# Cached attention on one core: from four 128-block tiles a head in five slots to three tiles of 172, 172 and 168 blocks in four

## The chip, the core and the metric

The kernel runs on one core of a Trainium2 chip. Five engines work side by side: TensorE (PE; its weight loads are listed as PEld), VectorE (DVE), ScalarE (ACT), GpSimd (POOL) and SyncE (SP). Here SP issues every load from HBM, in program order, and 16 DMA engines carry each one out. On-chip memory is SBUF, with 128 partitions, and PSUM, into which TensorE sums. The metric is the device time of one execution in microseconds, lower is better. The kernel before takes 2544.31 us, the median of three runs (2544.15 to 2545.1).

## The reference, cut to what matters

One token attends to a cache of 65,536 keys in each of 32 heads of 128 dimensions. A small feed-forward network runs beside it, and a sigmoid gate mixes the two.

```python
q = (x @ wq).reshape(B, Sq, H, Dh).transpose(0, 2, 1, 3)        # B = Sq = 1, H = 32, Dh = 128
scores = jnp.einsum("bhqd,bhkd->bhqk", q, k_cache) * (Dh ** -0.5)
p = _softmax(scores, axis=-1)
o = jnp.einsum("bhqk,bhkd->bhqd", p, v_cache)
a = o.transpose(0, 2, 1, 3).reshape(B, Sq, H * Dh) @ wo
b = (_silu(x @ w_gate) * (x @ w_up)) @ w_down                   # 512 -> 1792 -> 512
g = _sigmoid((x * gate_w).sum(-1, keepdims=True))
out = g * a + (1 - g) * b
```

All inputs are bfloat16. The two caches hold 32 x 65,536 x 128 x 2 bytes each, 537 MB; they are nearly all of the 1,087.6 MB that the kernel reads.

## The kernel before

**Tiles.** A head's 65,536 keys are 512 blocks of 128. A tile is `NB` = 128 blocks, so a head has `G` = 4 tiles for K and 4 for V, 4 MB each, and there are `N` = 128 tiles of each kind. A partition holds 128 consecutive keys of a tile, one contiguous run of 32,768 bytes in HBM and in SBUF. The function `big` hands out tiles from a pool of `SLOTS` = 5 slots. The load of a tile has to wait until whatever read the slot's last contents is done. `load` (lines 105 to 112) issues one transfer a tile; the last four V tiles go in two halves, the very last in pieces of 64, 32, 16 and 16 blocks (`CUTS`).

**Scores of a K tile.** `products` (210 to 227) is VectorE work, in place: one multiplication of the whole tile by the head's query (line 220), then three additions (line 224) that fold the 128 products of a key to 64, 32 and 16 columns. `scores` (229 to 241) lets TensorE sum the remaining `WIDTH` = 16 columns: 16 matmuls with an identity as weights, each over 128 numbers that lie 256 bytes apart, all into one slice of the PSUM tile `S_ps`, which holds the head's 512 blocks of scores.

**Softmax.** When a head's four tiles are scored, `row_max` (243) takes the maximum of each partition on VectorE, and a diagonal matrix and a matmul bring these maxima together; `exponentials` (253) takes the maximum over all, and ScalarE writes the weights `P_sb` and their sums. `total` and `weight` make the factor of the head.

**Values of a V tile.** `values` (276 to 289): 32 matmuls of four weight columns against 512 columns of V, summed into `O_ps`. `head_out` picks the diagonal out of it, `project` (326) multiplies with four heads' rows of wo, loaded in 512 KB pieces by `load_wo`.

**Order.** It is written by hand. The list `steps` (336 to 344) pairs each K tile n with a V tile v that comes four tiles behind; from `SPREAD` = 40 on, every fourth step leaves its V tile out until V is `LAG` = 8 tiles behind. In each step SP gets the load of K tile n and then of V tile v; VectorE gets the products of tile n, which at a head's first tile are cut into two halves, with `row_max` after the first instruction of the first half and `exponentials` after the second; TensorE gets the values of tile v and then the scores of tile n. At the start, wq and two K tiles are loaded, the queries are computed, then come the feed-forward weights in two slots and the first part of wo. The feed-forward itself is cut into three pieces in steps 1, 2 and 3. After the last step, `last_values` (291) works through the last V tile piece by piece, and the result is projected, cast and stored (389 to 399).

Of the kernel before, what the change touches and what calls it, by code (L numbers as in the profile page):

```python
# [15 lines left out]
NB = 128  # L16
SLOTS = 5
# [3 lines left out]
LAG = 8  # L21
SPREAD = 40

CUTS = (0, 64, 96, 112, 128)
# [3 lines left out]
def kernel(  # L28
# [23 lines left out]
    G = Sk // (NB * P)  # L52
    NBH = Sk // P
    N = H * G
    QG = 4
    assert Dh == P and Sk % (NB * P) == 0 and NBH <= 512 and H % QG == 0 and G >= 2
# [3 lines left out]
    ring = ctx.enter_context(tc.tile_pool(name="ring", bufs=SLOTS))  # L60
# [9 lines left out]

    def big(name):
        return ring.tile([P, NB * Dh], bf16, name=name, tag="big")

# [6 lines left out]
    wq_t = big("wq_t")  # L80
# [22 lines left out]
    K_tiles, V_tiles, S_tiles, P_tiles, O_tiles = {}, {}, {}, {}, {}  # L103

    def load(dst, cache, n, name, cuts=(0, NB)):
        h, g = divmod(n, G)
        t = big(name)
        view = t.rearrange("p (j d) -> p j d", d=Dh)
        src = cache[0, h, g * NB * P : (g + 1) * NB * P, :].rearrange("(p j) d -> p j d", j=NB)
        for a, b in zip(cuts[:-1], cuts[1:]):  # L110
            nc.sync.dma_start(out=view[:, a:b, :], in_=src[:, a:b, :])
        dst[n] = view
# [20 lines left out]


    gu_t = big("gu_t")
    wgu_sb = gu_t[:, : 2 * KT * F].rearrange("p (w t f) -> p w t f", w=2, t=KT)
    nc.sync.dma_start(out=wgu_sb[:, 0], in_=B_w_gate.rearrange("(p t) f -> p t f", t=KT))
    nc.sync.dma_start(out=wgu_sb[:, 1], in_=B_w_up.rearrange("(p t) f -> p t f", t=KT))
    wd_t = big("wd_t")
    wd_sb = wd_t[:, : FT * D].rearrange("p (t n) -> p t n", t=FT)  # L140
# [31 lines left out]
    def feed_forward_mid(gu_sb, eg):  # L172
        nc.vector.tensor_scalar_add(eg, eg, 1.0)
        nc.vector.reciprocal(eg, eg)
        hprod = consts.tile([P, FT], f32, name="hprod")
        nc.vector.tensor_tensor(out=hprod, in0=gu_sb[:, :FT], in1=eg, op=ALU.mult)
        hT = consts.tile([P, FT], bf16, name="hT")
        nc.vector.tensor_tensor(out=hT, in0=hprod, in1=gu_sb[:, FT:], op=ALU.mult)  # L178
        xg = consts.tile([P, KT], f32, name="xg")
        nc.vector.tensor_tensor(out=xg, in0=xT, in1=gwT, op=ALU.mult)  # L180
        xs = consts.tile([P, 1], f32, name="xs")
        nc.vector.tensor_reduce(out=xs, in_=xg, axis=AXIS.X, op=ALU.add)
        b_ps = psum_m.tile([1, D], f32, name="b_ps", tag="misc")
        for ft in range(FT):
            nc.tensor.matmul(  # L185
                b_ps,
                lhsT=hT[:, ft : ft + 1],
                rhs=wd_sb[:, ft, :],
                start=(ft == 0),
                stop=(ft == FT - 1),  # L190
            )
        g_ps = psum_m.tile([P, 1], f32, name="g_ps", tag="misc")
        nc.tensor.matmul(g_ps, lhsT=ones_f, rhs=xs, start=True, stop=True)
        eg2 = consts.tile([P, 1], f32, name="eg2")
        nc.scalar.activation(out=eg2, in_=g_ps, func=ACT.Exp, scale=-1.0)
        return b_ps, eg2
# [12 lines left out]

    def products(n, a=0, b=NB):  # L210

        h = n // G
        K = K_tiles[n][:, a:b, :]
# [15 lines left out]
    def scores(n):  # L229
        h, g = divmod(n, G)  # L230
        if g == 0:
            S_tiles[h] = psum_s.tile([P, NBH], f32, name="S_ps")
        for c in range(WIDTH):
            nc.tensor.matmul(  # L234
                S_tiles[h][:, g * NB : (g + 1) * NB],
                lhsT=ident_b,
                rhs=K_tiles[n][:, :, c],
                start=(c == 0),
                stop=(c == WIDTH - 1),
            )  # L240
        del K_tiles[n]
# [34 lines left out]
    def values(n):  # L276

        h, g = divmod(n, G)
        if g == 0:
            O_tiles[h] = psum_o.tile([4, 4 * Dh], f32, name="O_ps")  # L280
        for j in range(0, NB, 4):
            nc.tensor.matmul(  # L282
                O_tiles[h],
                lhsT=P_tiles[h][:, g * NB + j : g * NB + j + 4],
                rhs=V_tiles[n][:, j : j + 4, :],
                start=(g == 0 and j == 0),
                stop=(j == NB - 4 and (n == N - 2 or g == G - 1)),
            )
        del V_tiles[n]

    def last_values(oh_ps, a, b):

        h, g = divmod(N - 1, G)
        for j in range(a, b):
            nc.tensor.matmul(
                oh_ps,
                lhsT=V_tiles[N - 1][:, j, :],
                rhs=P_tiles[h][:, g * NB + j : g * NB + j + 1],
                start=(j == 0),
                stop=(j == NB - 1),  # L300
# [37 lines left out]
    for n in range(N):  # L338
        due = n >= G and not (n >= SPREAD and n % 4 == 3 and n - v < LAG)
# [7 lines left out]
    for n, v in steps:  # L347
        if n is not None and n > 1:
            load(K_tiles, A_k_cache, n, "K_t")
        if v is not None:  # L350
            if v % (WG * G) == 2 * G and v // (WG * G) + 1 < H // WG:
                load_wo(v // (WG * G) + 1)
            halves = (0, NB // 2, NB) if v >= N - G else (0, NB)
            load(V_tiles, A_v_cache, v, "V_t", CUTS if v == N - 1 else halves)
        vector = iter(()) if n is None else products(n)
        top_of = None
        if n is None:
            top_of = H - 1 if S_tiles else None
        elif n % G == 0 and n > 0:
            top_of = n // G - 1  # L360
            vector = (i for a in (0, NB // 2) for i in products(n, a, a + NB // 2))
        if top_of is not None:
            next(vector, None)
# [5 lines left out]
        if n == 1:  # L369
            ff = feed_forward_in()  # L370
        if n == 2:
            ff = feed_forward_mid(*ff)
        if n == 3:
# [10 lines left out]
        if n is not None:  # L384
            scores(n)
        if done is not None:
# [43 lines left out]
```

## Time and profile before

| what | value |
|---|---|
| median of three runs | 2544.31 us (2544.15 to 2545.1) |
| the profiled execution, its own time | 2544.7 us |
| span of its trace, first to last instruction | 2542.9 us |
| read from HBM | 1087.64 MB, 428 GB/s over the span |
| mean granted TensorE clock | 0.752 |
| K loads (4,096 KB) | 128, median 35.3 us from issue to landing |
| V loads (4,096 KB) | 124, median 29.7 us from issue to landing |
| VectorE idle before line 220 | 275.3 us in total, 256.0 of it ended by a K load |
| TensorE idle before line 282 | 499.6 us in total, 497.4 of it ended by a V load |

The page of the profile gives for each engine its busy time, its share of the span and the number of its instructions; then the DMA queues with packets, megabytes and the time of their packets as a share of 16 engines' span; then the chain of work that ended last, followed back from the end. A group line reads: source line, engine, operation, out<-in, partitions x elements, count | busy us in total, mean ns of one | idle us of the engine just before them, and what ended most of it. A window line reads: start:end, length, busy us (and instructions) of PE, PEld, DVE, ACT and POOL, then the granted clock, the share of DMA time and GB/s. A timeline line reads: start us, duration us, engine, line, operation, out<-in, shape, count, and in brackets the idle time before it. "SPq" is SP's queue, which issues the loads.

The trace also keeps each DMA packet with start, duration and size, and for every load the moment at which each of the 16 engines marks its share as landed.

### The profile page before, as it was taken

What the parts mean: (1) busy time and instruction counts of PE and PEld (TensorE: products, weight loads), DVE (VectorE), ACT (ScalarE), POOL (GpSimd) and SP (SyncE); (2) the same over time, 40 slices, a digit from 0 to 9 for tenths busy, and PEclk for the clock granted to TensorE, in tenths of its full rate; (3) what the DMA queues carried; (4) which work ended last, traced back from release to release, by engine and by line L of the source; (5) the groups of instructions that cost most, each with busy time, mean ns of one, the idle gap of its engine ahead of it and who ended that gap; (6) DMA issues with size and microseconds to landing.
All of it is one profiled execution on the core that took longest, in us unless ns stands there. A gap on an engine that the chain in (4) does not pass through costs nothing.

```text
span 2542.9 us, 15396 instructions
## 1 busy us (share of the span) xinstructions
PE 1721.1 (68%) x6818; PEld 705.6 (28%) x6818; DVE 2174.6 (86%) x779; ACT 75.9 (3%) x206; POOL 0.7 (0%) x6
## 2 busy tenths in 40 slices
PE   3576766766677656667676676667666676677768
PEld 2232222222222222222232222222222222222223
DVE  6999888888888999998888888888888888888870
ACT  1000000000000000000000000000000000000000
POOL 0000000000000000000000000000000000000000
PEclk7677777777777677776777777777777777777779
DMA  9999999999999999999999999999999999999998
GB/s 408 427 432 430 432 430 432 431 429 431 431 432 430 429 432 431 431 432 431 429 431 431 432 429 430 432 430 431 429 432 432 430 432 428 433 431 431 432 431 348
DMA packets 42884, 1088.63 MB, mean 428 GB/s; under 512 B 4673, under 2 KB 8770, under 8 KB 9026
## 3 DMA queue, kind: packets, MB, share of 16 engines
q1 hardware_dynamic: 42818, 1087.66, 99.6%
q8 instruction: 53, 0.87, 0.1%
q14 instruction: 13, 0.11, 0.0%
HBM read 1087.64 MB, written 0.00 MB: 428 GB/s over the span
## 4 chain that ended last, share of the span: by engine, by line
DMA 68%; PE 21%; DVE 11%; issue 1%; ACT 0%; SPq 0%; DVEq 0%
DMA V_t<-in_A_v_cache_dram 63%; PE O_ps L282 19%; DVE K_t L220 6%; DVE K_t L224 5%; DMA K_t<-in_A_k_cache_dram 4%; PE S_ps L234 1%; DMA wq_t<-in_A_wq_dram 0%; PE qg_ps L120 0%; DVE m L246 0%; PE oh_ps L308 0%; PE a_ps L207 0%; ACT P_sb L259 0%; DVE top L255 0%; ACT O_sb L306 0%; PE a_ps L327 0%
## 5 line engine op out<-in xcount | busy, mean ns | idle before, releaser
L282 PE MATMUL O_ps<-V_t,P_sb 128*4 128x512 bf16 x4064 | 1139.3, 450 | 499.6 <-DMA V_t<-in_A_v_cache_dram 497.4
L220 DVE TENSOR_TENSOR K_t<-K_t,q_bc 128x16384 bf16<-128x16384 bf16 (+1 forms) x159 | 1117.2, 7026 | 275.3 <-DMA K_t<-in_A_k_cache_dram 256.0
L224 DVE TENSOR_TENSOR K_t<-K_t 128x2048 bf16<-128x2048 bf16 (+3 forms) x477 | 1030.6, 2161 | 14.2
L282 PEld LDWEIGHTS <-P_sb 128*4 128x4 bf16 x4064 | 389.4, 96 | 1229.9 <-issue 883.3
L234 PE MATMUL S_ps<-K_t,ident_b 128*128 128x128 bf16 x2048 | 464.6, 392 | 123.8 <-DVE K_t L224 123.8
L234 PEld LDWEIGHTS <-ident_b 128*128 128x128 bf16 x2048 | 225.6, 114 | 346.9 <-issue 153.1
L308 PE MATMUL oh_ps<-ident_f,O_sb 4*128 4x1 f32 x256 | 57.2, 340 | 74.0 <-ACT O_sb L306 74.0
L250 PE MATMUL mT_ps<-diag,ones_f 128*128 128x128 f32 x64 | 23.6, 468 | 80.8 <-ACT diag L248 80.8
L308 PEld LDWEIGHTS oh_ps<-ident_f,O_sb 4*128 4x128 f32 x256 | 54.5, 310 | 83.1 <-ACT O_sb L306 78.8
L248 ACT ACTIVATE diag<-ident_f,m 128x128 f32<-128x128 f32 x32 | 12.8, 401 | 2108.3 <-DVE m L246 2108.3
L398 DVE CAST out_sb<-a_ps 1x512 bf16<-1x512 f32 x1 | 0.7, 677 | 52.4 <-PE a_ps L327 52.4
L250 PEld LDWEIGHTS mT_ps<-diag,ones_f 128*128 128x128 f32 x64 | 14.8, 288 | 96.6 <-ACT diag L248 96.6
L246 DVE TENSOR_REDUCE m<-S_ps 128x1 f32<-128x512 f32 x32 | 21.9, 684 | 7.4 <-PE S_ps L234 7.4
L259 ACT ACTIVATE P_sb<-S_ps,bias 128x512 bf16<-128x512 f32 x32 | 22.0, 687 | 1.0
L306 ACT ACTIVATE O_sb<-O_ps 4x512 f32<-4x512 f32 x32 | 18.3, 573 | 123.1 <-PE O_ps L282 123.1
L120 PE MATMUL qg_ps<-wq_t,X_bc 128*128 128x512 bf16 x32 | 8.5, 431 | 14.1 <-DMA wq_t<-in_A_wq_dram 14.1
L185 PE MATMUL b_ps<-wd_t,hT 128*1 128x512 bf16 x14 | 5.7, 597 | 15.7 <-DVE hT L178 15.7
L273 DVE RECIPROCAL recip<-tot_ps 128x1 f32<-128x1 f32 x32 | 5.1, 160 | 12.2 <-PE tot_ps L268 12.2
L327 PE MATMUL a_ps<-wo_sb,oT 128*1 128x512 bf16 x32 | 13.5, 423 | 0.4 <-ACT oT L317 0.4
L268 PEld LDWEIGHTS tot_ps<-rowsum,ones_f 128*128 128x128 f32 x64 | 9.5, 188 | 14.0 <-issue 14.0
L268 PE MATMUL tot_ps<-rowsum,ones_f 128*128 128x1 f32 x64 | 12.2, 260 | 0.0
L317 ACT ACTIVATE oT<-oh_ps,rg 128x1 bf16<-128x1 f32 x32 | 8.4, 264 | 81.2 <-PE oh_ps L308 75.0
(39 smaller groups left out, 69.1 us busy)
## 6 DMA issues: line engine op xcount, KB each, us to landing
K_t<-in_A_k_cache_dram SPq DMA_DIRECT2D x128, 4096.0 KB, 35.3
V_t<-in_A_v_cache_dram SPq DMA_DIRECT2D x124, 4096.0 KB, 29.7
V_t<-in_A_v_cache_dram SPq DMA_DIRECT2D x7, 2048.0 KB, 31.8
wq_t<-in_A_wq_dram SPq DMA_DIRECT2D x1, 4096.0 KB, 12.4
wo_sb<-in_A_wo_dram SPq DMA_DIRECT2D x8, 512.0 KB, 36.6
gu_t<-in_B_w_gate_dram SPq DMA_DIRECT2D x1, 1792.0 KB, 34.7
gu_t<-in_B_w_up_dram SPq DMA_DIRECT2D x1, 1792.0 KB, 38.4
wd_t<-in_B_w_down_dram SPq DMA_DIRECT2D x1, 1792.0 KB, 42.2
```

Source lines behind the costliest of these rows:

```text
L220: yield nc.vector.tensor_tensor(out=K, in0=K, in1=q_rep, op=ALU.mult)
L224: yield nc.vector.tensor_tensor(out=K[:, :, 0:half], in0=K[:, :, 0:half], in1=K[:, :, half : 2 * half], op=ALU.add,)
L234: nc.tensor.matmul(S_tiles[h][:, g * NB : (g + 1) * NB], lhsT=ident_b, rhs=K_tiles[n][:, :, c], start=(c == 0), stop=(c == WIDTH - 1),)
L246: nc.vector.tensor_reduce(out=m, in_=S_tiles[h], axis=AXIS.X, op=ALU.max)
L248: nc.scalar.activation(out=diag, in_=ident_f, func=ACT.Copy, scale=m)
L250: nc.tensor.matmul(mT_ps, lhsT=ones_f, rhs=diag, start=True, stop=True)
L259: nc.scalar.activation(out=P_tiles[h], in_=S_tiles[h], func=ACT.Exp, bias=bias, scale=scale, accum_out=rowsum[:, h : h + 1],)
L268: nc.tensor.matmul(tot_ps, lhsT=ones_f, rhs=rowsum[:, h : h + 1], start=True, stop=True)
L282: nc.tensor.matmul(O_tiles[h], lhsT=P_tiles[h][:, g * NB + j : g * NB + j + 4], rhs=V_tiles[n][:, j : j + 4, :], start=(g == 0 and j == 0) ...
L306: nc.scalar.activation(out=O_sb, in_=O_tiles.pop(h), func=ACT.Copy)
L308: nc.tensor.matmul(oh_ps, lhsT=O_sb[:, c * Dh : (c + 1) * Dh], rhs=ident_f[0:4, c : c + 1], start=(alone and c == 0), stop=(alone and c == 3),
L327: nc.tensor.matmul(a_ps, lhsT=oT[:, h : h + 1], rhs=wo_tiles[h // WG][:, h % WG, :], start=False, stop=(h == H - 1),)
```

## The change

A head is cut into three tiles of 172, 172 and 168 blocks, so N becomes 96, and a partition's run of a tile 44,032 or 43,008 bytes. There are four slots of 44,032 bytes a partition in place of five of 32,768. Slots are taken from the list `free`, to which the code returns a slot where TensorE has had its last instruction on it. The feed-forward weights share one slot.

TensorE sums two neighbouring columns at a time: 8 matmuls a tile in place of 16, each over up to 344 numbers (two side by side, then a step of 256 bytes), into a PSUM tile `S2_ps` of its own for each K tile. A new VectorE step, `fold`, adds the two sums of each block and writes them to `S_sb`, which now lies in SBUF. It comes one step later, after the first instruction of the next tile's products. At a head's first tile the products are cut at 72 blocks. The feed-forward's pieces move up to the end of step 0 and to steps 1 and 2. V falls back from 3 to `LAG` = 6 tiles, one V tile left out every sixth step from step 30 on. The last three V tiles are loaded in pieces of 88 and 84 blocks, the last of them in 88, 40, 24 and 16.

```diff
-NB = 128
-SLOTS = 5
+SIZES = (172, 172, 168)
+SLOTS = 4
 WIDTH = 16
-LAG = 8
-SPREAD = 40
-CUTS = (0, 64, 96, 112, 128)
+FIRST = 72
+LAG = 6
+SPREAD = 30
+HALVES = (0, 88)
+CUTS = (0, 88, 128, 152, 168)
...
+    free = list(range(SLOTS))
     def big(name):
-        return ring.tile([P, NB * Dh], bf16, name=name, tag="big")
+        slot = free.pop(0)
+        return slot, ring.tile([P, NB * Dh], bf16, name=name, tag=f"slot{slot}")
...
+    free.append(wq_slot)
-    gu_t = big("gu_t")
+    ff_slot, ff_t = big("ff_t")
...
     def scores(n):
-        for c in range(WIDTH):
-            nc.tensor.matmul(
-                S_tiles[h][:, g * NB : (g + 1) * NB],
-                lhsT=ident_b,
-                rhs=K_tiles[n][:, :, c],
-                start=(c == 0),
-                stop=(c == WIDTH - 1),
-            )
-        del K_tiles[n]
+        nb = SIZES[n % G]
+        slot, K = K_tiles.pop(n)
+        S2_tiles[n] = psum_s.tile([P, 2 * NB], f32, name="S2_ps")
+        for c in range(0, WIDTH, 2):
+            nc.tensor.matmul(
+                S2_tiles[n][:, : 2 * nb],
+                lhsT=ident_b,
+                rhs=K[:, :, c : c + 2],
+                start=(c == 0),
+                stop=(c == WIDTH - 2),
+            )
+        free.append(slot)
+
+    def fold(n):
         h, g = divmod(n, G)
+        nb = SIZES[g]
         if g == 0:
-            S_tiles[h] = psum_s.tile([P, NBH], f32, name="S_ps")
+            S_tiles[h] = small.tile([P, NBH], f32, name="S_sb")
+        S2 = S2_tiles.pop(n)
+        nc.vector.tensor_reduce(
+            out=S_tiles[h][:, AT[g] : AT[g] + nb],
+            in_=S2[:, : 2 * nb].rearrange("p (j c) -> p j c", c=2),
+            axis=AXIS.X,
+            op=ALU.add,
+        )
...
     def values(n):
-        for j in range(0, NB, 4):
+        slot, V = V_tiles.pop(n)
+        for j in range(0, SIZES[g], 4):
...
-        del V_tiles[n]
+        free.append(slot)
...
-        due = n >= G and not (n >= SPREAD and n % 4 == 3 and n - v < LAG)
+        due = n >= G and not (n >= SPREAD and n % 6 == 3 and n - v < LAG)
...
         elif n % G == 0 and n > 0:
             top_of = n // G - 1
-            vector = (i for a in (0, NB // 2) for i in products(n, a, a + NB // 2))
+            vector = (
+                i for a, b in ((0, FIRST), (FIRST, SIZES[0])) for i in products(n, a, b)
+            )
+        else:
+            vector = products(n, 0, SIZES[n % G])
+        next(vector, None)
+        if S2_tiles:
+            fold(min(S2_tiles))
         if top_of is not None:
-            next(vector, None)
             mT_ps = row_max(top_of)
             next(vector, None)
             exponentials(top_of, mT_ps)
         for _ in vector:
             pass
         if n == 1:
-            ff = feed_forward_in()
+            ff = feed_forward_mid(*ff)
         if n == 2:
-            ff = feed_forward_mid(*ff)
-        if n == 3:
             feed_forward_out(*ff)
...
         if n is not None:
             scores(n)
+        if n == 0:
+            ff = feed_forward_in()
```

## The prediction

> **What bounds the kernel now.** I read the page first, then the busy time by window, then the DMA records one by one, then the first 130 us and the last 25 of the timeline. The page:
>
> ```profile
> span 2542.9 us, 15396 instructions
> PE 1721.1 (68%) x6818; PEld 705.6 (28%) x6818; DVE 2174.6 (86%) x779; ACT 75.9 (3%) x206; POOL 0.7 (0%) x6
> ...
> q1 hardware_dynamic: 42818, 1087.66, 99.6%
> q8 instruction: 53, 0.87, 0.1%
> ...
> DMA 68%; PE 21%; DVE 11%; issue 1%; ACT 0%; SPq 0%; DVEq 0%
> ```
>
> The load queue (q1) keeps all 16 DMA engines occupied for 99.6% of the span. VectorE at 86% and TensorE at 68% have room. Where is the remaining 0.4%?
>
> ```profile
> 120.00:2520.00 2400.00, 1650.56 (x6343) 670.45 (x6341) 2081.33 (x738) 66.08 (x186) 0.00 (x0) 0.76 1.00 431
> ...
> 2520.00:2530.00 10.00, 8.95 (x43) 3.47 (x41) 0.00 (x0) 0.00 (x0) 0.00 (x0) 1.00 0.84 354
> 2530.00:2535.00 5.00, 3.74 (x70) 2.19 (x69) 0.00 (x0) 0.59 (x1) 0.00 (x0) 1.00 0.52 214
> ```
>
> The last two columns are DMA share and GB/s. From 120 to 2520 us the loads run at 431 GB/s without a pause; then the share falls to 0.84 and 0.52, because the 16 engines do not finish together. The load's bytes do not change, so the new time is set by three things: the cost of a byte and of a transfer, how far the slowest engine trails, and any moment when the queue runs dry.
>
> **Cost of a transfer.** In the trace's DMA records (one row a packet, and one landing mark for each engine of a transfer) a 4 MB load is 8 packets of 32,768 B on each engine. On the engine that lands first, successive 4 MB loads land 9.71 us apart (216 of them 9.71 or 9.72), 2 MB halves 4.89, 1 MB 2.49, 512 KB 1.265. Twice 4.893 less 9.7145 leaves **0.0715 us fixed a transfer** (8 packets of about 8.9 ns); the bytes cost 4.8215 us per 2 MB. That line gives 2.48 and 1.28 for the two small sizes, so it holds from 4 to 32 KB a packet. A 172-block tile (44,032 B a packet) is then 12.958 + 0.0715 = 13.03 us, a 168-block tile 12.73. K and V take 128 + 134 = 262 transfers before and 96 + 101 = 197 after: 65 x 0.0715 = **4.65 us less**. Lower bound 0, if the fixed part grows with the packet.
>
> The Trainium skill (DMA: Bandwidth & Descriptors, Anatomy of one DMA) puts about 2.0 us fixed on each DMA. By that, 65 fewer would be 130 us less. The landings 9.71 us apart deny it: queued loads overlap everything but 0.07 us.
>
> **Instruction fetches.** The 53 packets of queue q8 (16 KB each, about every 48 us, 0.94 to 1.11 us long) use the same engines. Where one falls, one engine's next landing comes 11.25 us after its last instead of 9.71: it loses 1.54 us. Their lengths repeat with period 8, so they go round eight engines. The spread between first and last engine is 0.5 us at 14 us, 1.9 at 86, 3.1 at 203, 4.7 at 428, 6.2 at 878, 7.7 at 1220, 9.2 at 1678, 10.9 at 2019, 12.4 from 2477 on: the engine of fetches 0, 8, ... 48 sets the end, 12.4 us after the first. TensorE's program shrinks from 13,096 to 10,597 instructions (the two programs' listings; 8 pairs a K tile in place of 16: 768 score matmuls for 2048). 53 fetches for 14,769 instructions of all engines give about 43 for 12,080. The slow engine then has 6 (0, 8, ... 40), not 7: **1.54 us less**. Bounds: 0, and 3.1 if only 40 come or the extra 1.6 us that this engine lost at 117 us does not recur.
>
> The skill (Runtime: NRT & Kernel Launch, Instruction fetch mechanics) calls the cost of a 16 KiB boundary "mostly hidden". By it this term is 0 and the sum 4.65. The trace's steps of 1.54 us speak against it.
>
> **VectorE.** Rows by shape:
>
> ```profile
> L220 DVE TENSOR_TENSOR K_t<-K_t,q_bc 128x16384 bf16<-128x16384 bf16 x97 | 843.1, 8691 | 208.3 <-DMA K_t<-in_A_k_cache_dram 191.7 <-PE O_ps L282 16.6
> L224 DVE TENSOR_TENSOR K_t<-K_t 128x8192 bf16<-128x8192 bf16 x97 | 429.2, 4425 | 3.3
> L224 DVE TENSOR_TENSOR K_t<-K_t 128x4096 bf16<-128x4096 bf16 x159 | 364.1, 2290 | 4.4
> ...
> L246 DVE TENSOR_REDUCE m<-S_ps 128x1 f32<-128x512 f32 x32 | 21.9, 684 | 7.4 <-PE S_ps L234 7.4
> ...
> L255 DVE TENSOR_REDUCE top<-mT_ps 128x1 f32<-128x128 f32 x32 | 9.1, 285 | 1.0 <-PE mT_ps L250 1.0
> ```
>
> 4425 to 2290 ns is 0.521 ns an element and 0.155 us fixed. 172 blocks: 11.63 + 5.89 + 3.02 + 1.59 = 22.13 us; 168: 21.6. The fold is new: 344 fp32 from PSUM, between the reduces of 128 (0.285) and 512 (0.684); 1.04 ns an element gives 0.51. A head is 2 x 22.13 + 21.6, four more adds where the first tile is cut (0.62), three folds 1.53, row_max and the rest 1.3: 69.3 us. Its six transfers take 4 x 13.03 + 2 x 12.73 = 77.6. VectorE stays 8.3 us a head under the DMA, so its work is priced at 0. That cover goes only if a fold with its wait costs above 0.51 + 8.3/3 = 3.3 us.
>
> **TensorE.** A score matmul comes every 217 ns for 128 columns 256 B apart, in both clock phases. For pairs the trace has no row: 8 x 0.29 = 2.3 us a tile if a pair costs one column's time, 8 x 0.58 = 4.7 if each column pays. Before it would be 16 x 0.29 = 4.7 for as many blocks, so it cannot get worse by these rows; I take 4.7. The fold waits for these scores with all later VectorE work behind it, but has the product ahead of it as cover: 11.6 us, or 4.96 for the 72 blocks at a head's start, against 4.7. TensorE's values keep eight matmuls at 427 ns and the rest at 216: 43 take 11.0 us of a 26.06 us pair.
>
> **Slots.** Four slots with two used a step means K of step n waits for the values of step n-2, V for the scores of step n-2. With K landing at T, those values end by T + 13 + 11 = T + 24, and the load that needs the slot starts at T + 39; issue to first packet is 1.07 us (issue at 113.80, first packet 114.87). So 14 us of backlog are covered, and V has more: 0. SP issues in order, a late K also holds the V behind it, and both were counted. The tight place is the start:
>
> ```profile
> 76.62 5.74 PE L185 MATMUL b_ps<-wd_t,hT 128*1 128x512 bf16 x14 [15.70 <-DVE hT L178]
> ...
> 82.39 0.33 SPq L111 DMA_DIRECT2D K_t<-in_A_k_cache_dram  x1
> ...
> 104.35 9.42 PE L282 MATMUL O_ps<-V_t,P_sb 128*4 128x512 bf16 x32 [2.22 <-ACT P_sb L259]
> ```
>
> The first engine now lands K0 at 26.6, K1 39.6, the feed-forward weights 52.5, wo 54.0, K2 66.7, K3 79.7 (a packet ends 0.46 before its landing: 114.87 and 115.33). VectorE starts at 27.15; K0 to 49.3, K1 with one fold to 72.0, hT 0.91 later, b_ps 5.77: the slot for V0 comes at 78.7, its packets at 79.8, against 79.25. Half a microsecond is lost on fast engines and none on the slow one, which trails by 1.9. The feed-forward's three steps come one K tile earlier: its six small VectorE operations (1.04 us) now stand before K2's product, and b_ps with the two gate matmuls before the scores of K1, which end at 78.7 + 0.4 + 4.7 = 83.8. K4 waits for them; its packets are due at 92.8. V1 waits for the scores of K2, 95.2 + 4.7 = 99.9, and is due at 105.8. Both lie hidden. Next, K2 to 95.2, out of the feed-forward 95.7, 72-block product and fold 101.2, maximum, one add, top 104.7, exponentials 105.8, 43 values (9.42 + 11 x 0.216) 117.6: K5 is issued there and V1's packets end at 118.9. It just fits. If the clock kept all 43 values at 427 ns (18.4 us), K5 would be 6.4 us late, 4.5 beyond the slow engine's lag; if the fold equals the 128-element row, it gains 0.4. I take **0**, range 0 to +4.5.
>
> **The end.** The last piece stays 16 blocks; the chain behind its landing is unchanged: 0.
>
> **Sum.** -4.65 - 1.54 + 0 = -6.2: the profiled execution (2544.7 us, span 2542.9) becomes 2538.5; the median of the runs, 2544.31, lies 0.4 below it, so 2538.1.
>
> **Rivals.** (A) Only part arrives: fetches stay hidden or a start gap of 1 to 4.5 us eats it. For it: two start slacks near zero. Against: both were built from rows. 4.65 less 4.5 to 4.65 less 0: 2539.7 to 2544.2, centre 2541.5. (B) Slower: the rows of 44,032 B do not go as one packet. No packet above 32,768 B is in the trace; cut in two, each transfer costs 0.143, 197 x 0.143 - 262 x 0.0715 = +9.4, less 1.54: 2552.2. It decides from the first load on, and the packet sizes would show it. Against: every contiguous row so far went as one packet. The skill's DMA page (Why a DMA increments its semaphore by 16) implies a limit of 64 KiB a descriptor; no run here shows it. (C) Slower by VectorE: each 0.1 us of fold above 3.3 us costs 9.6; a 3.5 us fold gives +20, 2558. Against: five times the longest reduce row.
>
> **How the numbers follow.** Forecast 0.65, a better end spread (-9.3: 2535.0) 0.04, A 0.17, B 0.06, C and other starvation 0.08. What the measurement can tell from no change is about 0.2%, 5.1 us. The forecast is beyond it; most of A lies within. Faster 0.65 + 0.04 = 0.69, same 0.17, slower 0.06 + 0.08 = 0.14. The range goes from 2535.0 (both fetch bounds) to 2543.5 (most of A).
>
> **What would show it.** Right: landings 13.03 us apart, packets of 44,032 B, some 43 q8 packets, a last spread near 10.9 us, DVE near 2200 us, fold near 0.5 us, SP waits ending with slack after 130 us. Wrong: two packet sizes a row, a DMA share below 0.98 after 130 us, a gap of over 2 us near 80 or 119 us, a fold over 3 us, a spread still 12 us or more.

## The result, and the profile after

| | before | after |
|---|---|---|
| median, 13 runs each | 2543.89 us (2542.86 to 2545.1) | 2538.02 us (2536.95 to 2540.06) |
| profiled execution, its own time | 2544.7 us | 2538.62 us |
| its span | 2542.9 us | 2536.8 us |
| last landing of a load, first engine | 2526.09 us | 2521.85 us |
| last landing of a load, last engine | 2538.47 us | 2532.32 us |

The ratio is 0.9978 with a 95% interval of 0.9971 to 0.9986. Predicted were 2538.1 us and a span of 2536.7. The gain of 5.9 us is small, but the interval is clear of no change. The question left is whether the time went for the reasons given. "First engine" and "last engine" are, for each load, the one of the 16 DMA engines that marks its share as landed first and the one that does so last; the spread is the time between them.

The page of the kernel after, the same lines as were shown of before:

```profile
span 2536.8 us, 12707 instructions
...
PE 1433.4 (57%) x5568; PEld 553.4 (22%) x5568; DVE 2192.0 (86%) x747; ACT 77.2 (3%) x206; POOL 0.7 (0%) x6
...
q1 hardware_dynamic: 33458, 1087.65, 99.6%
q8 instruction: 43, 0.70, 0.1%
...
DMA 64%; PE 23%; DVE 12%; issue 1%; ACT 0%; SPq 0%; DVEq 0%
```

The bytes of q1 are the same and its share of the span is the same 99.6%; only its packets went from 42,818 to 33,458, and the fetches of q8 from 53 to 43. VectorE and the chain by engines are nearly unchanged. TensorE lost 288 us of work and the kernel six: TensorE was not what set the time. The windows:

```profile
120.00:2520.00 2400.00, 1378.54 (x5134) 526.07 (x5133) 2098.40 (x707) 67.33 (x186) 0.00 (x0) 0.74 1.00 432
2520.00:2530.00 10.00, 9.14 (x143) 5.72 (x142) 0.00 (x0) 0.59 (x1) 0.00 (x0) 1.00 0.64 266
2530.00:2535.00 5.00, 2.60 (x65) 1.84 (x61) 0.68 (x1) 0.26 (x1) 0.00 (x0) 0.50 0.05 21
```

The rate went from 431 to 432 GB/s with no pause in 2,400 us. The end shows the same picture six microseconds earlier: the share falls to 0.64 in the ten microseconds in which before still had 0.84, since engines run out one after another.

In the trace's DMA records a packet of a 172-block tile is 44,032 bytes, one for each partition's row, and the 172-block landings of the first engine mostly come 13.02 or 13.03 us apart, those of 168 blocks 12.72 or 12.73.

### The profile page after: what moved, and what is told of

It is laid out like the page before. It is cut to its first block, busy times and chain, and to the rows that moved or that the text cites. A ratio compares the mean times of both kernels' runs of the same rounds, so it can differ in the third digit from the quotient of the medians.

```text
span 2536.8 us, 12707 instructions
## 1 busy us (share of the span) xinstructions
PE 1433.4 (57%) x5568; PEld 553.4 (22%) x5568; DVE 2192.0 (86%) x747; ACT 77.2 (3%) x206; POOL 0.7 (0%) x6
## 3 DMA queue, kind: packets, MB, share of 16 engines
q1 hardware_dynamic: 33458, 1087.65, 99.6%
## 4 chain that ended last, share of the span: by engine, by line
DMA 64%; PE 23%; DVE 12%; issue 1%; ACT 0%; SPq 0%; DVEq 0%
DMA V_t<-in_A_v_cache_dram 59%; PE O_ps L310 18%; DVE K_t L237 6%; DVE K_t L233 6%; DMA K_t<-in_A_k_cache_dram 4%; PE S_ps L248 4%; DVE S_sb L263 0%; PE tot_ps L295 0%; DVE m L273 0%; PE a_ps L220 0%; PE oh_ps L336 0%; SPq L122 0%; DVE top L282 0%; PE a_ps L355 0%; ACT P_sb L286 0%
## 5 line engine op out<-in xcount | busy, mean ns | idle before, releaser
L310 PE MATMUL O_ps<-V_t,P_sb 128*4 128x512 bf16 x4054 | 1073.5, 433 | 659.6 <-DMA V_t<-in_A_v_cache_dram 657.1
L233 DVE TENSOR_TENSOR K_t<-K_t,q_bc 128x21504 bf16<-128x21504 bf16 (+2 forms) x127 | 1112.0, 8756 | 260.7 <-DMA K_t<-in_A_k_cache_dram 260.7
L237 DVE TENSOR_TENSOR K_t<-K_t 128x10752 bf16<-128x10752 bf16 (+2 forms) x381 | 1014.6, 2663 | 8.8
L310 PEld LDWEIGHTS <-P_sb 128*4 128x4 bf16 x4054 | 379.3, 94 | 1340.4 <-issue 948.4
L248 PE MATMUL S_ps<-K_t,ident_b 128*128 128x344 bf16 (+1 forms) x768 | 236.5, 463 | 134.0 <-DVE K_t L237 133.9
L248 PEld LDWEIGHTS <-ident_b 128*128 128x128 bf16 x768 | 79.8, 114 | 263.1 <-issue 148.2
L263 DVE TENSOR_REDUCE S_sb<-S_ps 128x172 f32<-128x344 f32 (+1 forms) x96 | 48.5, 506 | 4.3 <-PE S_ps L248 4.3
L286 ACT ACTIVATE P_sb<-S_sb,bias 128x512 bf16<-128x512 f32 x32 | 23.1, 722 | 1.0
L273 DVE TENSOR_REDUCE m<-S_sb 128x1 f32<-128x512 f32 x32 | 22.0, 686 | 1.1
L295 PEld LDWEIGHTS tot_ps<-rowsum,ones_f 128*128 128x128 f32 x64 | 10.1, 199 | 18.3 <-issue 9.6
```

Of the source, the lines that this page charges most:

```text
L233: yield nc.vector.tensor_tensor(out=K, in0=K, in1=q_rep, op=ALU.mult)
L237: yield nc.vector.tensor_tensor(out=K[:, :, 0:half], in0=K[:, :, 0:half], in1=K[:, :, half : 2 * half], op=ALU.add,)
L248: nc.tensor.matmul(S2_tiles[n][:, : 2 * nb], lhsT=ident_b, rhs=K[:, :, c : c + 2], start=(c == 0), stop=(c == WIDTH - 2),)
L263: nc.vector.tensor_reduce(out=S_tiles[h][:, AT[g] : AT[g] + nb], in_=S2[:, : 2 * nb].rearrange("p (j c) -> p j c", c=2), axis=AXIS.X, op=A ...
L273: nc.vector.tensor_reduce(out=m, in_=S_tiles[h], axis=AXIS.X, op=ALU.max)
L286: nc.scalar.activation(out=P_tiles[h], in_=S_tiles[h], func=ACT.Exp, bias=bias, scale=scale, accum_out=rowsum[:, h : h + 1],)
```

## The experiments

The theory: the change gains by fewer packets (4.65 us) and by one instruction fetch fewer on the engine that ends last (1.54 us), and nothing else counts. The rivals: the fixed cost belongs to the transfer and not to its packets; the fetches cost nothing and the end spread has another cause; the start, or VectorE's new work, gave something back. All kernels are the kernel after with the edit shown, except where it says before; `...` marks code left out. "Beside" is the ratio to the kernel before on the same chip, with its interval.

| kernel | median us | beside |
|---|---|---|
| two_transfers | 2551.71 | 1.0032 (1.0019 to 1.0044) |
| two_runs | 2551.68 | 1.0033 (1.0021 to 1.0045) |
| before_pairs | 2541.79 | 0.9994 (0.9985 to 1.0003) |
| more_instructions | 2546.3 | 1.0013 (1.0004 to 1.0022) |
| single_columns | 2539.2 | 0.9982 (0.9973 to 0.9991) |
| ff_late | 2555.66 | 1.0047 (1.0034 to 1.0061) |
| fold4 | 2545.26 | 1.0006 (0.9997 to 1.0016) |
| early | 2536.67 | 0.9973 (0.9963 to 0.9983) |
| even_end | 2561.51 | 1.0069 (1.0057 to 1.0082) |
| after_again (after, a second time) | 2537.41 | 0.9975 (0.9966 to 0.9984) |
| early_again (early, a second time) | 2537.05 | 0.9974 (0.9964 to 0.9984) |

### What a transfer costs, and whether the transfer or the packet costs it

`two_transfers` loads every tile in two halves, as two transfers:

```diff
-    def load(dst, cache, n, name, cuts=(0,)):
+    def load(dst, cache, n, name, cuts=HALVES):
...
-            cuts = CUTS[:-1] if v == N - 1 else HALVES if v >= N - G else (0,)
+            cuts = CUTS[:-1] if v == N - 1 else HALVES
```

> The changed kernel, but every K and V tile loaded by two transfers (88 blocks and the rest): 189 more transfers of the same bytes, nothing else moved. Theory (a transfer costs 0.0715 us fixed on the DMA engines, which set the time): +189 x 0.0715 = +13.5 us, about 2551.5 us, parts landing 6.70 and 6.40 us apart on the engine that lands first. Rival (the gain came from fewer instructions or from the finer end, not from fewer transfers): 2538 us, no change from the changed kernel.

`two_runs` keeps one transfer a tile but lets it consist of two runs for each partition, so that it has the packets of two halves and the landing mark of one transfer:

```diff
+        if n < N - G:
+            half = SIZES[g] // 2
+            nc.sync.dma_start(
+                out=view.rearrange("p (s j) d -> p s (j d)", s=2),
+                in_=keys.rearrange("(s p j) d -> p s (j d)", s=2, j=half),
+            )
+            dst[n] = slot, view
+            return
```

> The changed kernel, but in the first 186 K and V loads a partition takes its keys as two runs of half the length, in one transfer (16 packets of 22,016 or 21,504 B an engine in place of 8; the keys lie on other partitions, the same for K and V, so the sums are the same). If the fixed 0.0715 us belongs to the eight packets (8.9 ns each): +186 x 0.0715 = +13.3 us, about 2551.3 us, 172-block tiles 13.10 us apart. If it belongs to the transfer and its landing marks: 2538 us, tiles 13.03 us apart.

The queue lines of the page, first of `two_transfers`, then of `two_runs`:

```profile
DMA packets 60732, 1088.48 MB, mean 427 GB/s; under 512 B 6658, under 2 KB 10755, under 8 KB 11011
...
q1 hardware_dynamic: 60674, 1087.66, 99.9%
q8 instruction: 43, 0.70, 0.1%
```

```profile
DMA packets 57321, 1088.45 MB, mean 427 GB/s; under 512 B 3633, under 2 KB 7730, under 8 KB 7986
...
q1 hardware_dynamic: 57266, 1087.65, 99.9%
q8 instruction: 43, 0.70, 0.1%
```

Both have the 43 fetches and the bytes of the kernel after. `two_runs` has 23,808 packets more (186 tiles x 128), `two_transfers` 27,216 (189 x 128, and 3,024 more packets under 512 bytes, which are 16 landing marks for each of 189 transfers). The times are 13.7 us above the kernel after in both. In `two_transfers` the first engine's last landing comes at 2535.67 us, 13.8 us later than after, which is 0.073 us for each of 189; the halves of a 172-block tile land 6.70 and 6.40 us apart. In `two_runs` the same tiles land 13.10 and 12.80 us apart, 0.07 us more than in the kernel after, with one landing mark each. So the fixed cost of 0.0715 us belongs to the eight packets an engine carries of a tile, 8.9 ns each, and the landing marks of a transfer cost nothing that can be seen here. That is the larger term of the prediction, measured in the other direction.

The Trainium skill (DMA: Bandwidth & Descriptors, Anatomy of one DMA) gives a fixed part of about 2.0 us for a DMA on the GpSimd path; the prediction left that condition out, and here SP issues. 189 more of them would be 378 us by that figure; the run shows 13.7. Whether the figure holds for one transfer by itself no run here shows; behind other transfers in SP's queue it does not.

### Whether the instruction fetches set the end

`before_pairs` is the kernel before with one thing of the change: two neighbouring columns to a score matmul, and VectorE's addition of the two. Tiles, slots, transfers and the feed-forward's place are those of before.

```diff
-        for c in range(WIDTH):
+        for c in range(0, WIDTH, 2):
             nc.tensor.matmul(
-                S_tiles[h][:, g * NB : (g + 1) * NB],
+                S2_tiles[n],
                 lhsT=ident_b,
-                rhs=K_tiles[n][:, :, c],
+                rhs=K_tiles[n][:, :, c : c + 2],
...
```

> The kernel before, with its four 128-block tiles, five slots and order, and of the change only the paired columns on TensorE and the fold on VectorE. TensorE's program has 11,049 instructions in place of 13,096, so some 46 instruction fetches in place of 53, 6 on the engine that ends last in place of 7. Theory (a fetch costs that engine 1.54 us of loads): -1.5 us against the kernel before, 2542.4 us, spread of the engines at the end 10.9 us in place of 12.4. Rival (fetches are hidden, all of the gain is in the transfers): 2543.9 us, spread unchanged. Rival (the pairs and the fold free the engines and give most of the gain): 2539 us.

`more_instructions` adds 64 small matmuls with unused results behind the scores of each tile:

```diff
...
+        x_ps = psum_x.tile([P, 1], f32, name="x_ps")
+        for _ in range(64):
+            nc.tensor.matmul(x_ps, lhsT=ident_b, rhs=ident_b[:, 0:1], start=True, stop=True)
```

> The changed kernel with 64 further one-column matmuls on TensorE behind each K tile's scores, their results unused: 12,257 more instructions, 3.9 us a step of a TensorE that idles for 11, some 87 instruction fetches in place of 43, 11 in place of 6 on the engine that ends last. Theory: +5 x 1.54 = +7.7 us, about 2545.7 us, spread at the end about 18 us in place of 10.5. Rival (fetches are hidden): 2538 us, spread 10.5.

The page of `before_pairs`, then that of `more_instructions`:

```profile
span 2540.1 us, 13386 instructions
...
q1 hardware_dynamic: 42818, 1087.66, 99.7%
q8 instruction: 45, 0.74, 0.1%
```

```profile
span 2545.3 us, 24964 instructions
...
q1 hardware_dynamic: 33458, 1087.65, 99.4%
q8 instruction: 91, 1.49, 0.2%
```

`before_pairs` has the packets of before (42,818) and eight fetches fewer. The first engine's last landing comes where it came before (2525.66 us for 2526.09), the spread at the end falls from 12.4 to 9.98 us, and the median by 1.53 us. The ratio's interval reaches 1.0003, so the time by itself does not settle it. Nor does the spread at the end: in before a load issued at 113.80 us had lost 0.45 us on the first engine and 1.6 on the last, and in `before_pairs`, where it was issued at 113.29, it lost nothing. What the fetches do is read from the growth of the spread after about 145 us, where both starts are over: 9.3 us in before, which has 50 fetches after 140 us, and 7.9 in `before_pairs`, which has 43. In four executions of the kernel after and of `early` (below), with 41, it is 7.5 to 8.1. These are near six and five times the 1.54 us that the prediction read for a fetch.

`more_instructions` has the packets of the kernel after (33,458) and 48 fetches more, six on each of eight engines. The last landing moves from 2532.3 to 2540.8 us, 8.5 us or 1.4 us for each of the six; the median is 8.3 us up. TensorE's busy time grew by 165 us in it and still ended far below VectorE's. Where the expectation was wrong is the place: it had the spread grow to 18 us, but it is 11.7, and the first engine also lands 7.2 us later than in the kernel after. A slot is free, and a tile usable, only when all sixteen engines have landed their share, so the fast engines can get ahead by no more than the slots let them. The timeline of `more_instructions` has such a place: the values that begin at 1731.40 us had made TensorE wait 11.4 us for their V tile, whose landings run from 1718.83 to 1731.36; the K load that needs their slot is issued behind them at 1742.72, and lands 13.6 us after the load ahead of it on the first engine in place of 13.03, and 13.0 on the last. TensorE was idle before these values, so there the added matmuls were not what held the load up. How much of the 7.2 us comes about in this way was not tried by itself.

The skill (Runtime: NRT & Kernel Launch, Instruction fetch mechanics) calls the cost of a 16 KiB boundary "mostly hidden". From the issuing engine's side nothing here speaks against that; on the DMA engines that also carry the loads, a fetch cost the engine that ends last about 1.4 us (`more_instructions`) to 1.54 us (the steps of before).

`single_columns` gives every score matmul one column again, with the tiles, slots and order of the kernel after, and a copy of the sums in place of the fold:

```diff
-        for c in range(0, WIDTH, 2):
+        for c in range(WIDTH):
             nc.tensor.matmul(
-                S2_tiles[n][:, : 2 * nb],
+                S2_tiles[n][:, :nb],
                 lhsT=ident_b,
-                rhs=K[:, :, c : c + 2],
+                rhs=K[:, :, c],
...
+        nc.vector.tensor_copy(out=S_tiles[h][:, AT[g] : AT[g] + nb], in_=S2[:, :nb])
```

> The changed kernel without the pairs: 16 matmuls of one column each a K tile, and a plain copy from PSUM to SBUF in place of the fold. TensorE has 12,102 instructions, so 48 or 49 fetches in place of 43, one more on the engine that ends last if there are 49; a tile's scores take 4.7 us in place of 2.5, and K5's load is issued about 2 us later. Theory: +1.5 us or 0 for the fetches, +1 to 2 us for the start: 2539 to 2541.5 us, spread at the end 10.5 to 12 us. Rival (the pairs are worth nothing here): 2538 us.

Its page has `x6336` matmuls for 5568 and 49 fetches for 43, and its median stands 1.2 us above the kernel after; the intervals of the two ratios overlap. The time by itself thus proves nothing. The spread at the end is 10.4 us, no more than the kernel after's 10.5; but at 145 us it was 1.1 where the kernel after had 2.7, and from there it grew by 9.3 us, with 47 fetches after 140 us for 41. That is one step more, as in before.

Fetches do not explain every lag. In the kernel after seven engines end within 2.3 us of the first and eight 7.7 to 10.5 us after it; one more ends 6.9 us after it, and no run shows why.

### Whether the start gave anything back

`ff_late` puts the feed-forward's three pieces back into steps 1, 2 and 3, where before had them:

```diff
         if n == 1:
-            ff = feed_forward_mid(*ff)
+            ff = feed_forward_in()
         if n == 2:
+            ff = feed_forward_mid(*ff)
+        if n == 3:
             feed_forward_out(*ff)
...
-        if n == 0:
-            ff = feed_forward_in()
```

> The changed kernel with the feed-forward's three pieces where the kernel before has them (steps 1, 2, 3). Theory (with four slots the start hangs on when the feed-forward gives up its slot and its place in TensorE's order): K4 waits for b_ps behind K2's products, about 99.8 us against packets that end at 92.2, 8 to 9 us late; the gate's end then stands ahead of the first values, which end some 15 us later than now, and K5 comes 8 to 11 us late again: +16 us in all (13 to 20), about 2554 us. Rival (loads in flight cover it, the move is worth nothing): 2538 us.

The timeline of the kernel after at the first two waits for a slot (columns: start, duration, engine, line, operation, tiles, shape, count):

```profile
72.63 4.74 PE L197 MATMUL b_ps<-ff_t,hT 128*1 128x512 bf16 x14 [14.08 <-DVE hT L190]
...
77.40 0.33 SPq L122 DMA_DIRECT2D V_t<-in_A_v_cache_dram  x1
...
77.55 2.49 PE L248 MATMUL S_ps<-K_t,ident_b 128*128 128x344 bf16 x8
...
105.29 11.73 PE L310 MATMUL O_ps<-V_t,P_sb 128*4 128x512 bf16 x43 [2.52 <-ACT P_sb L286]
...
117.05 0.33 SPq L122 DMA_DIRECT2D K_t<-in_A_k_cache_dram  x1
```

And that of `ff_late`:

```profile
94.84 4.88 PE L197 MATMUL b_ps<-ff_t,hT 128*1 128x512 bf16 x14 [20.24 <-DVE hT L190]
...
99.75 0.33 SPq L122 DMA_DIRECT2D K_t<-in_A_k_cache_dram  x1
...
124.45 11.68 PE L310 MATMUL O_ps<-V_t,P_sb 128*4 128x512 bf16 x43
136.17 0.33 SPq L122 DMA_DIRECT2D K_t<-in_A_k_cache_dram  x1
```

With four slots the feed-forward's shared slot is due for a cache load earlier: in before the load behind `b_ps` was that of K5, at 82.39 us, here it is that of V0, at 77.40. In `ff_late` TensorE's `b_ps` comes 22 us later, the K load behind it is issued at 99.75, the one after the first 43 values at 136.17 for 117.05. In the DMA records the first engine lands these two loads 21.97 and 23.12 us after the ones ahead of them, in place of 13.03 and 12.73: 8.9 and 10.4 us in which the queue was dry. The whole kernel is 17.6 us longer. So the early place of the feed-forward was worth that much, and the prediction was right to count the start in tenths.

The kernel after itself is not quite free of a loss there. V0's load, issued at 77.40 with 1.75 us in hand before the packets ahead of it end, cost nothing. K5's, issued at 117.05, had 1.2 us in hand (V1's packets end at 118.23 on the first engine), and yet it landed 14.02 us after V1 instead of 12.73, and 14.82 on the last engine: 1.3 and 2.1 us lost. The packets show no gap, as K5's first one begins at 118.23; but most of those that begin before 120.8 us last 2.0 to 2.8 us in place of the usual 1.59. When the kernel after was profiled a second time (`after_again`), the places had changed: K5 was issued at 116.36, with 2.6 us in hand, and lost nothing (12.74), while V0 was issued at 78.40, with 0.9 us in hand, and landed 13.62 us after the load ahead of it instead of 13.03, 0.6 us lost on the first engine and none on the last. So the start loses something in both, and how much changes from one execution to the next.

`early` loosens K5's place: the last piece of the feed-forward moves behind the scores of tile 2, and the first piece of tile 3's products is 48 blocks in place of 72, so that the maximum comes sooner.

```diff
+            first = 48 if n == G else FIRST
...
-        if n == 2:
-            feed_forward_out(*ff)
...
+        if n == 2:
+            feed_forward_out(*ff)
```

> The changed kernel with two steps of the start moved: the gate's end (its a_ps matmul) goes behind the scores of K2 in place of ahead of them, and the first head's softmax starts after 48 blocks of products in place of 72. The load of K5 should be issued 2 to 2.5 us sooner, at about 114.7 us. Theory (in the changed kernel K5 comes with 1.2 us in hand, and its landing 14.02 us after V1's in place of 12.73 is a restart of the queue, on the engine that ends last 2.1 us): K5 lands 12.73 us after V1, 1.3 to 2.1 us less, about 2536.3 us. Rival (the engines that end last trail by more than the gap, so it costs nothing): 2538 us.

The timeline of `early` at the same place:

```profile
102.63 11.41 PE L310 MATMUL O_ps<-V_t,P_sb 128*4 128x512 bf16 x43 [1.72 <-ACT P_sb L286]
...
114.07 0.33 SPq L122 DMA_DIRECT2D K_t<-in_A_k_cache_dram  x1
```

The load is issued 3 us sooner and lands 12.72 us after V1: nothing is lost at K5. V0's place stays as tight as it was: in the second execution of `early` it was issued at 77.83, with 1.2 us in hand, and lost 0.3 us on the first engine and 0.9 on the last. The median was 2536.67 us. Both kernels were then run beside each other once more:

> The changed kernel once more, on the same chip beside the version with the earlier K5 load and the one with the evened end: 2538 us, spread of the engines at the end 10.5 us.

> The version with the earlier K5 load once more beside the changed kernel: 2536.7 us, 1.3 us below the changed kernel if the restart at K5 is what it takes away; equal to it if the difference of the first two lay in the chips.

Side by side they are 2537.41 and 2537.05 us, with overlapping ranges. The expected spread of 10.5 us did not come: it was 9.0 in this execution of the kernel after, which lost nothing at K5, and 10.3 in that of `early`. So one profiled spread at the end is good to some 1.5 us. `early` is not slower, but a gain over the kernel after of more than some tenths of a microsecond is not shown.

### How much VectorE could take

The prediction held that a fold may cost up to 3.3 us before VectorE decides. `fold4` makes each fold four times (the same result each time):

```diff
-        nc.vector.tensor_reduce(
+        for _ in range(4):
+            nc.vector.tensor_reduce(
...
```

> The changed kernel with each fold done four times (the same result again): VectorE 1.53 us more a K tile, 73.9 us a head under 77.6 us of loads. As the prediction had it, VectorE costs nothing until a fold is above 3.3 us: 2538 us. Rival (the start has no slack: V0 and K5 come 1.5 and 4.6 us later and the queue runs dry there, the rest is covered): +4 to 5 us, 2542.5 us. Rival (the steps that leave a V tile out, between 850 and 1260 us, also build up more VectorE backlog than the slots cover): over 2545 us, with gaps in the loads after 130 us.

The prediction was wrong here: 2545.26 us, 7.2 above the kernel after, as the last rival had it, with losses at the start as the first rival had them. Three more folds of 0.51 us are 1.53 us a tile, so one fold and its copies stand at 2.05, well below 3.3. The windows say where; columns as above, VectorE's is the third busy time. The kernel after:

```profile
400.00:860.00 460.00, 265.59 (x975) 100.86 (x976) 406.11 (x138) 12.95 (x36) 0.00 (x0) 0.73 1.00 432
860.00:1290.00 430.00, 226.16 (x845) 87.74 (x844) 409.15 (x139) 12.54 (x34) 0.00 (x0) 0.70 1.00 432
```

And `fold4`:

```profile
400.00:860.00 460.00, 260.35 (x957) 98.80 (x957) 432.27 (x190) 12.94 (x36) 0.00 (x0) 0.74 1.00 432
860.00:1290.00 430.00, 221.74 (x844) 87.45 (x842) 424.18 (x188) 12.54 (x34) 0.00 (x0) 0.70 0.99 427
```

From 400 to 860 us the kernel after keeps VectorE busy for 88% of the time, from 860 to 1290 for 95%. In that stretch every sixth step leaves its V tile out, so K tiles follow each other faster. Two heads then bring 6 K and 5 V transfers, 142.1 us by the landings (1003.41 to 1145.49 us), against VectorE's 2 x 69.3 = 138.6 by the prediction's sum: 3.5 us of room for six folds, 0.6 us each, not the 2.8 that the mean over a head gives. By the timeline of the kernel after, where VectorE goes through a head without a wait in 68.5 us (1033.20 to 1101.74), it is 0.8. `fold4` asks for 1.53 more and fills VectorE to 98.6%. The timeline of `fold4` shows how it reaches the loads:

```profile
1241.69 0.69 DVE L274 TENSOR_REDUCE m<-S_sb 128x1 f32<-128x512 f32 x1
...
1242.86 0.80 PE L278 MATMUL mT_ps<-diag,ones_f 128*128 128x128 f32 x2 [5.63 <-ACT diag L276]
...
1248.44 10.99 PE L311 MATMUL O_ps<-V_t,P_sb 128*4 128x512 bf16 x43
...
1259.47 0.33 SPq L122 DMA_DIRECT2D K_t<-in_A_k_cache_dram  x1
```

The maximum's matmul stands on TensorE ahead of the values, and waits for VectorE's `m`; the values then end at 1259.4, and the K load that needs their slot goes out at 1259.47. It lands 16.62 us after the load ahead of it in place of 13.02: 3.6 us lost. Another 2.7 us go at 1204 us, and at the start V0 and K5 land 14.32 and 16.54 us after their forerunners, 1.3 and 2.5 us above the kernel after. These four are 10.1 us on the first engine. The last engine loses less (its last landing comes 6.3 us later), because each pause lets the slow engines catch up: the spread at 1313 us is 1.8 us where the kernel after has 6.3.

### Whether the engines could be made to end together

At the end of the kernel after seven engines are done 4.6 to 10.5 us before the other nine. `even_end` (with the edit of `early`) is meant to give the slow engines' share of one late V tile to others, by cutting its first 106 blocks into one transfer of 64 partitions and eight of 8 partitions:

```diff
+        if dst is V_tiles and n == N - G:
+            X = 106
+            eights = [slice(r, r + 8) for r in range(64, P, 8)]
+            for rows in eights[:4] + [slice(0, 64)] + eights[4:]:
+                nc.sync.dma_start(out=view[rows, :X, :], in_=src[rows, :X, :])
+            cuts = (X,)
...
```

> The version with the earlier K5 load, and one V tile (the third from the end) loaded differently: 106 of its blocks in eight transfers of 8 partitions for partitions 64 to 127, and one of 64 partitions for the rest. The Trainium skill (DMA: Bandwidth & Descriptors, Why a DMA increments its semaphore by 16 and not by 1) has a transfer of 8 rows run on the eight lowest-numbered engines; no run here has shown it. Each of these eight then carries 4.0 us more, the other eight 4.0 us less. Theory (the engines that lose to instruction fetches end last and set the time, 7 to 10 us behind the others): if those are the upper eight, the spread at the end falls from 9.9 to about 3 us and the time by some 4 us, to 2532.7 us; if they are the lower eight, the spread grows to about 18 us and the time by 4 us, to 2540.7 us. Rival (the engines' spread does not set the end): 2536.7 us, plus some tenths for nine more transfers.

The kernel became slower, 24 us above the kernel after on the same chip (2537.41). The windows of `even_end`:

```profile
2400.00:2480.00 80.00, 52.55 (x192) 19.57 (x192) 57.04 (x19) 2.16 (x6) 0.00 (x0) 0.75 1.00 433
2480.00:2520.00 40.00, 25.56 (x114) 10.07 (x112) 0.33 (x2) 0.85 (x2) 0.00 (x0) 0.84 0.94 215
2520.00:2560.00 40.00, 28.38 (x264) 14.26 (x264) 0.68 (x1) 0.85 (x2) 0.00 (x0) 0.76 0.63 265
```

From 2480 to 2520 us the DMA share is 0.94 but the rate only half, 215 GB/s. The tile's 128 packets of 27,136 bytes, half of them of the 64-partition transfer and half of the small ones, lasted 1.4 to 2.7 us each, where by the cost of a byte in the large loads they should last 1.0. The loads issued behind them waited. Each small transfer left eight landing marks and one more about 0.5 us after its issue, where a load over 128 partitions leaves sixteen; that agrees with eight engines, but not which eight they are. Neither theory had foreseen the slow packets, and why they are slow was not tried. Whether an even end would bring the time forward is still open.

## Why the prediction was right, and where it was not

- **Transfers: -4.65 us.** Right in kind and size. The first engine's last landing moved by -4.24 us in the first profiled execution and by -4.70 in the second; the start took back some of it (K5's 1.3 us and V0's 0.6, where before had lost 0.45 at its own tight place). What the prediction left open, whether transfer or packet has the cost, is settled by `two_runs`: the packet.
- **Fetches: -1.54 us.** 43 fetches were predicted and came. The spread at the end fell by 1.9 us (12.4 to 10.5; 10.9 predicted), in the second execution by 3.4, so the 1.9 by itself is partly luck. The growth of the spread after 145 us is the better measure: 9.3 us before, 7.8 and 7.5 after, one step of 1.54 us less. `more_instructions` shows the term in the time, in the other direction.
- **TensorE: 0.** The upper end was taken, 4.7 us for a tile's scores. Eight matmuls took 2.49: two neighbouring numbers cost what one does. Over the kernel 512 matmuls of 344 numbers keep TensorE busy for 158.9 us, and in `single_columns` 1,024 of 172 numbers for 307.5. It was hidden either way.
- **VectorE: 0, with cover to 3.3 us a fold.** The price was right (0.51 us predicted, 508 ns measured for a 172-block fold in the row of line 263 below) and so was the 0. The cover was not. The step that failed divided a head's 8.3 us of room by three, and so took a head with all its V loads for every stretch of the kernel; at the start, and where V is left out, there is 0 to 0.8 us. `fold4` shows 7.2 us lost at 2.05 us a fold.
- **Slots: 0.** After 120 us the DMA share is 1.00. But of the "14 us of backlog" much is used: the tightest load after 130 us, issued at 2362.57, had 3.3 us in hand.
- **The start: 0, "just fits".** The two loads were issued at 77.40 and 117.05 us, where 78.7 and 117.6 were worked out (`b_ps` took 4.74 us for 5.77). It did not quite fit: the first engine lost 1.3 us in one profiled execution and 0.6 in the other, the last engine 2.1 and nothing. The kernel before had lost 0.45 and 1.6 at its own tight place, so against it the last engine loses 0.5 us or gains 1.6. The term's range, 0 to 4.5, had the loss; the gain stands among the bounds of the fetch term, as the 1.6 us that may not recur. In the second execution the last engine's last landing came 8.1 us before that of before: 4.65 and 1.54 and these 1.6 are 7.8. That the first execution came so close to the sum (6.15 us by the last landing, 6.2 predicted) is luck to that extent.
- **Rivals.** Of A, a loss at the start came, near the low end of its 1 to 4.5 us, but the kernel before had lost there too, so hardly any of it counts. B is excluded: rows of 44,032 bytes went as one packet. The skill (DMA: Bandwidth & Descriptors, Why a DMA increments its semaphore by 16 and not by 1) was read as setting a limit of 64 KiB; these packets agree with it and do not test it. C did not occur, but lay nearer than its condition said.

The rows by shape of the kernel after that these points use:

```profile
L233 DVE TENSOR_TENSOR K_t<-K_t,q_bc 128x22016 bf16<-128x22016 bf16 x33 | 383.6, 11623 | 81.5 <-DMA K_t<-in_A_k_cache_dram 81.5
...
L263 DVE TENSOR_REDUCE S_sb<-S_ps 128x172 f32<-128x344 f32 x64 | 32.5, 508 | 0.0
```

VectorE still idles before a tile's multiplication because a K load has not landed, and never before a 172-block fold: the product ahead of it covers the scores.

## What to carry to other kernels

Where loads keep all DMA engines busy, cut the number of packets (longer rows, not merely fewer transfers) and the number of instructions, since their fetches take turns with the loads on some engines. Measure an engine's room in the stretch where it has least, at the start and wherever the mix of loads changes, and not by the mean of a period. A load that must not leave a gap should be issued well ahead of the end of the packets before it: at the start of these kernels 1.6 us and more were enough, and each of the loads with 1.2 us or less in hand (in before, `after`, `after_again`, `early_again`, `single_columns`, `two_runs` and `two_transfers`) lost 0.3 to 1.5 us on the first engine. In `more_instructions` loads with up to 2.2 us in hand still lost some tenths.

## What was not expected of the hardware

- Loading a tile by one transfer of 64 partitions and eight of 8, beside other loads, was slow for its bytes: packets of 27,136 bytes took 1.4 to 2.7 us, and the rate fell from 433 to 215 GB/s.
- A queue that has nearly run dry loses more than the gap that the issue times show: K5's first packet began at 118.23, as V1's packets ended on the first engine, and 1.3 us were still lost there and 2.1 on the last, in packets that lasted longer.
- Fetches hold back more than the engine that carries them: with 91 of them also the first engine landed its last load 7.2 us later.
